# A gated mix of a state-space scan and an MLP: the last output tile's stores, dealt out anew to two DMA queues

## The chip, the cores and the metric

The kernel runs on one core of one Trainium2 chip. The metric is the device time in microseconds of one execution; lower is better. Before the change it is 136.66 us, the median of three runs (136.61 to 136.97).

## The reference, cut to what matters

For one sequence of 2048 rows with 448 columns, the reference computes a state-space branch `a` (a complex diagonal recurrence with 448 states along the sequence, then an output projection), an MLP branch `b` (448 to 1792 and back, SiLU between), and mixes them row by row with a sigmoid gate:

```python
x = A_x
g = _sigmoid((x * gate_w).sum(-1, keepdims=True))
a = _A_ref(x, ...)   # h[t] = Lam_bar * h[t-1] + x[t] B_bar ;  y = 2 Re(C h) + x * Dskip
b = _B_ref(x, w1, w2)   # silu(x @ w1) @ w2
return g * a + (1 - g) * b
```

The output is bfloat16 of shape (1, 2048, 448), written row by row.

## The kernel before, in words

The sequence is treated as 1024 pairs of rows: `x2` and `out2` are views of 1024 x 896, where columns 0 to 447 are the even row of a pair and 448 to 895 the odd one. A block `kt` is 128 pairs, so there are 8 blocks and 16 output tiles `tile = 2 * kt + odd` of 128 partitions x 448 columns.

Every instruction is recorded by a small helper, the `Tracker`: `T.op` records a compute instruction, `T.dma` a transfer. Both work out, from the names of the buffers that an instruction reads and writes, which semaphores it has to wait for. The order on each engine is the order of these calls, written out by hand; there is no scheduler. Each transfer has a semaphore of its own. `T.wait_all("sp", outs)` at the end makes the SyncE (SP) engine wait for all output stores in the order in which they were recorded, and nothing comes after it. A transfer can be issued by SP's queue or by ScalarE's (`"act"`); ScalarE's own instructions and the transfers that it issues stand in one order.

The first part of the kernel loads the inputs, computes the MLP and the scans, and keeps the states in `HS` and `VE`. Then come the 16 output tiles. For each one:

- `yseed` (line 1041) lets ScalarE copy a start value into a bank of PSUM.
- `yhalf` (line 1049) adds seven matmuls of the states with the projection `CO`, `YA` five of them and `YB` two.
- `yout` (lines 1062 to 1079) applies the gate and adds the MLP's share, and stores the tile. For the first eight tiles (`kt < 4`) that is a ScalarE activation (line 1070), for the last eight a VectorE operation (`scalar_tensor_tensor`, line 1073). The result lies in one of eight output buffers; the profile names four of them `OT` and the other four `TMPS`. The store is line 1077.

Fifteen tiles are stored whole, by one transfer each on SP's queue. The sixteenth, the last one (`kt = 7`, even), is cut by columns: a first piece of 280 columns and a second of 168. Each piece has its own bank, its own seven matmuls, its own VectorE operation and its own store. The rule for the queue is in `yout`: a piece that begins at column 0 goes to `"sp"`, the other to `"act"`. The loop that does this stands at line 1225, right ahead of the final wait.

Of the kernel before, what the change touches and what calls it, by code (L numbers as in the profile page):

```python
# [19 lines left out]
D = 448  # L20
# [130 lines left out]
def gated_mix(nc, A_x, A_Lambda_re, A_Lambda_im, A_B_re, A_B_im, A_C_re, A_C_im, A_log_dt,  # L151
              A_Dskip, B_x, B_w1, B_w2, gate_w, out):
    with ExitStack() as ctx:
        E = ctx.enter_context
        T = Tracker(nc, ctx)

        def sb(name, shape, dtype):
            return E(nc.sbuf_tensor(name, list(shape), dtype))

        x2 = A_x[0].rearrange("(k i) d -> k (i d)", i=2)  # L160
        out2 = out[0].rearrange("(k i) d -> k (i d)", i=2)
# [16 lines left out]
        OT = sb("OT", [128, 4, D], BF16)  # L178
# [21 lines left out]
        def bs(tile):  # L200
            kt, odd = tile // 2, tile % 2
            if odd:
                return BT[:, :, :].rearrange("p j n -> p (j n)")[:, kt * D:(kt + 1) * D]
            if kt > 3:
                return (COS, SIN)[kt // 6][:, 0, (kt % 2) * D:(kt % 2 + 1) * D]
            return IOTA[:, :].bitcast(BF16)[:, kt * D:(kt + 1) * D]
# [6 lines left out]
        def xg(b):  # L213
            if b < 2:
                return CO[:, 4 * b:4 * b + 4, :], [f"CO{m}" for m in (range(4) if b == 0 else range(4, 7))]
            if b == 2:
                return OT[:, 0:4, :], [f"OT{i}" for i in range(4)]
            v = TMPS[:, :, :].rearrange("p a b -> p (a b)").bitcast(BF16)
            return v[:, 0:4 * D].rearrange("p (k c) -> p k c", k=4), [f"TMP{i}" for i in range(3)]
# [90 lines left out]
        for i, src in enumerate((A_B_re, A_B_im)):  # L310
# [12 lines left out]
            out=ID[:, :], in_=ID[:, :], pattern=[[-1, 128]], compare_op=ALU.is_equal, fill=0.0,  # L323
            base=0, channel_multiplier=1), reads=["ID"], writes=["ID"])
        T.op("pool", lambda e: e.iota(IOTA[:, :].bitcast(I32), pattern=[[1, NK]], base=0, channel_multiplier=0),
             writes=["IOTA"])
# [128 lines left out]
        def ffn1(c, f0=0, ahead=None):  # L455
            for fb in range(f0, NFB, 2):
                pair(*ffn1_pair(c, fb), last=(c == 3 and fb == NFB - 2))
                if ahead and fb == 8:
                    ahead()
                yield  # L460
# [58 lines left out]
        for k in (2, 3):  # L519
# [7 lines left out]
            reads=["pv", "ps7"], writes=["PV"])  # L527
# [30 lines left out]
        def pact(o, a, f, ra, scale=1.0, bias=0.0):  # L558
# [22 lines left out]
            reads=["f2"] + SGN, writes=["f2s"])  # L581
# [84 lines left out]
        for n in (32, 64):  # L666
            T.op("dve", lambda e, n=n: e.tensor_copy(GD[n:2 * n, :, :], GD[0:n, :, :]), reads=["GW", "DB"],
                 writes=["GW", "DB"])
# [7 lines left out]
             writes=["BTz"] + BTK[2:4])  # L676
# [361 lines left out]
        def yseed(kt, odd):  # L1038
            bank, tile = nxt(), 2 * kt + odd
            s = bs(tile) if kt < 4 else xd(tile)  # L1040
            T.op("act", lambda e: e.activation(ps[:, bank, 0:D], s, AF.Copy),
                 reads=[f"BS{tile}" if kt < 4 else f"XD{block(tile)}"], writes=[f"ps{bank}"])
            seeds.append((kt, odd, bank))

        def yhalf(ms, kt, odd, bank, c=slice(0, D)):
            def mm(pe):
                ins = None
                for m in ms:
                    ins = pe.matmul(ps[:, bank, c], state(kt, odd, m), CO[:, m, c], start=False, stop=(m == YB[-1]),  # L1049
                                    skip_group_check=True)  # L1050
                return ins
            T.op("pe", mm, reads=sk(kt, odd, ms) + [f"CO{m}" for m in ms], writes=[f"ps{bank}"])
            return kt, odd, bank
# [5 lines left out]
            yhalf(YB, kt, odd, bank)  # L1059
            return 2 * kt + odd, bank  # L1060

        def yout(tile, bank, c=slice(0, D)):
            kt, odd = tile // 2, tile % 2
            i = n_o[0] % 8
            n_o[0] += c.stop == D
            o = (OT[:, i, :] if i < 4 else xg(3)[0][:, i - 4, :])[:, c]
            extra = xg(3)[1] + ["CT4", "CT5", "CT6"] if n_o[0] == 5 else []
            g = GT[:, 1, tile:tile + 1]
            if kt < 4:
                T.op("act", lambda e: e.activation(o, ps[:, bank, 0:D], AF.Copy, scale=g),  # L1070
                     reads=[f"ps{bank}", "GT1_0"], writes=[f"OT{i}"] + extra)
            else:
                T.op("dve", lambda e: e.scalar_tensor_tensor(  # L1073
                    o, ps[:, bank, c], g, bs(tile)[:, c], ALU.mult, ALU.add),
                    reads=[f"ps{bank}", "GT1_1", f"BS{tile}"], writes=[f"OT{i}_{c.start}"] + extra + (
                        [f"OT{i}"] if c.start == 0 else []))
            outs.append(T.dma("act" if c.start else "sp", lambda e: e.dma_start(
                out2[kt * 128:(kt + 1) * 128, odd * D + c.start:odd * D + c.stop], o),
                reads=[f"OT{i}" if kt < 4 else f"OT{i}_{c.start}"], writes=[f"out{tile}_{c.start}"]))

        outs = []

# [80 lines left out]
        f = ffn1(2)  # L1163
# [48 lines left out]
        for _ in range(8):  # L1212
            t = yclose(*yopen())
            ahead()
            yout(*t)
        run(s2)
        opened = [yopen(), yopen(), yopen()]
        kt, odd = tiles[-1]
        for n in range(1, 8):
            ahead()  # L1220
            yout(*yclose(*opened.pop(0)))
            if n in (2, 3, 4, 6):
                opened.append(yopen())
        yseed(kt, odd)
        for c in (slice(0, 280), slice(280, D)):
            kt, odd, bank = seeds.pop(0)
            yhalf(YA + YB, kt, odd, bank, c)
            yout(2 * kt + odd, bank, c)
        T.wait_all("sp", outs)

        T.emit()
# [2 lines left out]
def bass_gated_mix__ssm_conv_s5__dense_activation_silu__prompt_kernel(nc, *args):  # L1234
    gated_mix(nc, *args)
# [28 lines left out]
```

## Time and profile before

| What | Value |
|---|---|
| Time, median of 3 runs | 136.66 us (136.61 to 136.97) |
| Span of the profiled execution, first to last instruction | 135.2 us |
| TensorE clock granted | 1.000 |
| PE busy | 131.8 us, 97% of the span |
| DVE (VectorE) busy | 115.6 us, 86% |
| ACT (ScalarE) busy | 93.8 us, 69% |
| POOL (GpSimd) busy | 15.9 us, 12% |
| Output stores on SP's queue | 16 (15 of 112 KB, one of 70 KB) |
| Output stores on ScalarE's queue | 1 of 42 KB |
| Issue to landing of these stores, median | 1.6 to 1.7 us |

The profile is one execution. The page gives its span, which runs from the first to the last instruction of any engine, waits included; it gives no total for that execution beside it. So the profiled execution's own time is the 135.2 us of the span, and the difference to the 136.66 us of the runs' median is what lies around it. PE is a matmul on TensorE, PEld a weight load, SPq and ACTq are transfers issued by the two queues. The issue of a transfer is an instruction with a duration; "landing" is when its semaphore has been counted up by all DMA engines.

### The profile page before, as it was taken

The page shows a single profiled execution, that of the slowest core. Times are in us where ns is not written, and L with a number is a line of the kernel's source. Part 1 is how long each engine was busy: PE and PEld are TensorE (multiplying, and loading weights), DVE is VectorE, ACT ScalarE, POOL GpSimd, SP SyncE. Part 2 cuts the span into 40 slices and gives each one's busy share as a digit, 9 for nine tenths or more (in the row PEclk, how much of TensorE's full clock was granted, in tenths as well). Part 3 has the DMA queues.
Part 4 walks back from the last instruction along what each step waited for, and adds up shares of the span by engine and source line. Part 5 has one row for each costly group of instructions (what it writes and reads, how often), then busy time and mean ns, then how long its engine had stood idle before and what let it go on. Part 6 is the DMA issues. An engine that isn't in the chain of part 4 may idle for free.

```text
span 135.2 us, 2632 instructions
## 1 busy us (share of the span) xinstructions
PE 131.8 (97%) x1072; PEld 65.4 (48%) x1073; DVE 115.6 (86%) x154; ACT 93.8 (69%) x146; POOL 15.9 (12%) x32
## 2 busy tenths in 40 slices
PE   7899999999999999999999999999999999999993
PEld 7444444444444554444445544445555555555552
DVE  1369999917899798999999999999999999994554
ACT  0459888899939999769999597797114437879200
POOL 7108349650000000000000000000000000000000
DMA  4999979898997220000222000000000000322123
GB/s 110 259 275 176 125 140 264 165 323 248 259 188 119 53 63 0 0 0 0 55 47 58 5 0 0 0 5 0 0 0 0 0 0 5 102 91 79 68 80 124
DMA packets 24736, 11.78 MB, mean 87 GB/s; under 512 B 16851, under 2 KB 24214, under 8 KB 24726
## 3 DMA queue, kind: packets, MB, share of 16 engines
q1 hardware_dynamic: 22996, 10.43, 33.4%
q10 hardware_dynamic: 1730, 1.20, 3.1%
q8 instruction: 8, 0.13, 0.4%
q14 instruction: 2, 0.02, 0.0%
HBM read 5.34 MB, written 1.84 MB: 53 GB/s over the span
## 4 chain that ended last, share of the span: by engine, by line
PE 94%; DMA 2%; DVE 1%; SPq 1%; issue 0%
PE ps L362 44%; PE ps L796 16%; PE ps L811 16%; PE ps L1049 15%; PE ps L430 3%; DMA XN<-in_A_x_dram 2%; PE ps L488 1%; DVE TMPS L1073 1%; SPq L226 1%; PE ps L444 1%; PE ps L469 0%
## 5 line engine op out<-in xcount | busy, mean ns | idle before, releaser
L362 PE MATMUL ps<-XT,W1E 64*128 64x512 bf16 x325 | 41.3, 376 | 0.0
L452 ACT ACTIVATE AT<-ps 128x1024 bf16<-128x1024 f32 x28 | 28.2, 1020 | 7.4 <-PE ps L362 7.2
L362 PEld LDWEIGHTS ps<-XT,W1E 64*128 64x128 bf16 x325 | 16.9, 94 | 19.1 <-ACT AT L452 0.3
L362 PE MATMUL ps<-XT,BT 64*128 64x512 bf16 x156 | 22.4, 376 | 0.0
L811 PE MATMUL ps<-W,AT 64*128 64x448 bf16 x224 | 21.5, 349 | 0.0
L796 PE MATMUL ps<-W,AT 128*128 128x448 bf16 x112 | 21.4, 353 | 0.0
L796 PEld LDWEIGHTS ps<-W,AT 128*128 128x128 bf16 x112 | 10.9, 98 | 10.5 <-issue 0.4
L811 PEld LDWEIGHTS ps<-W,AT 64*128 64x128 bf16 x224 | 10.9, 94 | 10.4
L840 ACT ACTIVATE BT<-ps,GT 128x448 bf16<-128x448 f32 x8 | 5.1, 634 | 13.2 <-PE ps L796 13.2
L896 DVE SCALAR_TENSOR_TENSOR HS<-VE,P,ps 128x512 bf16<-128x512 bf16 (+1 forms) x13 | 9.6, 781 | 3.8 <-PE ps L362 3.8
L362 PEld LDWEIGHTS ps<-XT,BT 64*128 64x128 bf16 x156 | 8.1, 94 | 9.4 <-DVE HS L896 0.4
L940 DVE TENSOR_TENSOR_SCAN G<-P,Q 128x1024 f32<-128x1024 f32 (+1 forms) x6 | 11.4, 1922 | 0.0
L1049 PE MATMUL ps<-CO,VE 128*128 128x448 bf16 (+2 forms) x63 | 11.1, 332 | 0.0
L1049 PE MATMUL ps<-CO,HS 128*128 128x448 bf16 x56 | 11.1, 352 | 0.0
L362 PE MATMUL ps<-XR,W1E 64*128 64x512 bf16 x25 | 9.2, 376 | 0.0
L1049 PEld LDWEIGHTS ps<-CO,VE 128*128 128x128 bf16 x63 | 6.0, 98 | 4.8
L1049 PEld LDWEIGHTS ps<-CO,HS 128*128 128x128 bf16 x56 | 5.5, 98 | 5.1
L893 DVE TENSOR_TENSOR Q<-G,COS 128x2048 bf16<-128x2048 f32 (+1 forms) x4 | 7.0, 1756 | 0.1
L893 DVE TENSOR_TENSOR Q<-G,SIN 128x2048 bf16<-128x2048 f32 (+1 forms) x4 | 7.0, 1752 | 0.0
L858 ACT ACTIVATE VE<-ps 128x1024 bf16<-128x1024 f32 x6 | 6.1, 1020 | 1.2 <-PE ps L362 1.2
L860 ACT ACTIVATE ps<-VE,P 128x1024 f32<-128x1024 bf16 x6 | 6.7, 1118 | 0.2
L896 DVE SCALAR_TENSOR_TENSOR VE<-HS,P,FP 128x512 bf16<-128x512 bf16 (+1 forms) x7 | 6.6, 977 | 0.1
(124 smaller groups left out, 181.0 us busy)
## 6 DMA issues: line engine op xcount, KB each, us to landing
W<-in_B_w_dram SPq DMA_DIRECT2D x2, 784.0 KB, 6.3
XN<-in_A_x_dram SPq DMA_DIRECT2D x1, 896.0 KB, 5.5
out_dram<-OT SPq DMA_DIRECT2D x8, 112.0 KB, 1.7
out_dram<-TMPS SPq DMA_DIRECT2D x7, 112.0 KB, 1.7
HS<-HS SPq DMA_DIRECT2D x4, 128.0 KB, 2.3
XN<-in_A_x_dram SPq DMA_DIRECT2D x1, 384.0 KB, 3.6
W1E<-in_B_w_dram SPq DMA_DIRECT2D x1, 256.0 KB, 5.6
W1E<-in_B_w_dram ACTq DMA_DIRECT2D x1, 256.0 KB, 5.6
```

The costliest lines, as they stand in the source:

```text
L362: ins = pe.matmul(ps[:, bank, :], w(p, j), xh(odd, h, j, p), start=start and j == js[0], stop=stop and j == js[-1], skip_group_check=seeded)
L430: T.op("pe", lambda pe, fb=fb, bank=bank, j=j, h=h, c=c: pe.matmul(ps[:, bank, c], W1E[:, j, ff(fb) * 128:(ff(fb) + 1) * 128], XT[:, j, c] ...
L452: T.op("act", lambda e: e.activation(a[:, fb:fb + n, :], ps[:, bank:bank + n, :], AF.Silu), reads=[f"ps{bank + i}" for i in range(n)], wri ...
L796: ins = pe.matmul(ps[:, bank, 0:D], a[:, fb, q * 128:(q + 1) * 128], W2[:, ff(fb), :], start=(first and fb == 0), stop=(fb == NFB - 1), sk ...
L811: ins = pe.matmul(ps[:, bank, 0:D], a[p, fb, q * 128:(q + 1) * 128], W2[p, ff(fb), :], start=(start and fb == 0), stop=(not start and fb = ...
L840: T.op("act", lambda e: e.activation(bs(tile), ps[:, bank, 0:D], AF.Copy, scale=sc), reads=[f"ps{bank}", "GT2" if h else "GRI"], writes=ks)
L858: T.op("act", lambda e: e.activation(VE[:, m:m + 2, hs], ps[:, b[0]:b[0] + 2, :], AF.Copy), reads=[f"ps{i}" for i in b], writes=vs)
L860: T.op("act", lambda e: e.activation(ps[:, o[0]:o[0] + 2, :], VE[:, m:m + 2, hs], AF.Copy, scale=c1("lr", pt)), reads=vs + ["lr"], writes= ...
L893: T.op("dve", lambda e: e.tensor_tensor(o, a, b, op), reads=reads, writes=writes)
L896: T.op("dve", lambda e: e.scalar_tensor_tensor(o, a, s, b, ALU.mult, ALU.add), reads=reads, writes=writes)
L940: T.op("dve", lambda e: e.tensor_tensor_scan(G[:, c, w], rb, Q1[:, c, w], init, ALU.mult, ALU.add), reads=[f"Q1{c}", "rr", f"G{c}"], write ...
L1049: ins = pe.matmul(ps[:, bank, c], state(kt, odd, m), CO[:, m, c], start=False, stop=(m == YB[-1]), skip_group_check=True)
```

## The change

The function that stores a tile takes a list of transfers, each with a queue and a range of rows; without it a tile is stored whole by SP's queue. For the last tile the list is given: its first piece (280 columns) is one transfer on ScalarE's queue, and its second (168 columns) is two transfers, rows 0 to 63 on SP's queue and rows 64 to 127 on ScalarE's. Both halves read what one VectorE operation writes, and wait for it. Each of the three has its own semaphore, and the final wait takes them in this order.

```diff
-        def yout(tile, bank, c=slice(0, D)):
+        def yout(tile, bank, c=slice(0, D), to=(("sp", 0, 128),)):
...
-            outs.append(T.dma("act" if c.start else "sp", lambda e: e.dma_start(
-                out2[kt * 128:(kt + 1) * 128, odd * D + c.start:odd * D + c.stop], o),
-                reads=[f"OT{i}" if kt < 4 else f"OT{i}_{c.start}"], writes=[f"out{tile}_{c.start}"]))
+            for eng, r0, r1 in to:
+                outs.append(T.dma(eng, lambda e, r0=r0, r1=r1: e.dma_start(
+                    out2[kt * 128 + r0:kt * 128 + r1, odd * D + c.start:odd * D + c.stop], o[r0:r1, :]),
+                    reads=[f"OT{i}" if kt < 4 else f"OT{i}_{c.start}"], writes=[f"out{tile}_{c.start}_{r0}"]))
...
-        for c in (slice(0, 280), slice(280, D)):
+        for c, to in ((slice(0, 280), (("act", 0, 128),)), (slice(280, D), (("sp", 0, 64), ("act", 64, 128)))):
             kt, odd, bank = seeds.pop(0)
             yhalf(YA + YB, kt, odd, bank, c)
-            yout(2 * kt + odd, bank, c)
+            yout(2 * kt + odd, bank, c, to)
```

## The prediction

> **What bounds the kernel now.** I read the chain of waits first, then the timeline of the last three microseconds, then busy time by stretch behind the last compute instruction. The page's chain:
>
> ```profile
> ## 4 chain that ended last, share of the span: by engine, by line
> PE 94%; DMA 2%; DVE 1%; SPq 1%; issue 0%
> ```
>
> TensorE sets the pace of nearly the whole span. The change touches no matmul and no VectorE instruction, so only the tail behind PE can move. The timeline from 132.5 us on (start, duration, queue or engine, line):
>
> ```profile
> 132.26 0.91 PE L1049 MATMUL ps<-CO,VE 128*128 128x280 bf16 x9
> ...
> 132.58 0.99 SPq L1077 DMA_DIRECT2D out_dram<-TMPS  x2
> 132.70 0.90 DVE L1073 SCALAR_TENSOR_TENSOR TMPS<-ps,GT,SIN 128x280 bf16<-128x280 f32 x2
> 133.63 0.38 ACTq L1077 DMA_DIRECT2D out_dram<-TMPS  x1
> ```
>
> PE ends at 133.17. The two VectorE pieces (280 and 168 columns, 0.51 and 0.39 us) run back to back to 133.60. SP issues the first piece's store at 133.24 (the second of its x2), ScalarE's queue the second's at 133.63. That is the last instruction of any engine that does work; the remaining 1.6 us are one DMA's way to DRAM, and SP waits for it:
>
> ```profile
> L1077 ACTq DMA_DIRECT2D out_dram<-TMPS x1: 379/379/379, 133.6 to 133.6; - x1
> ...
> DMA to landing us min/median/max: 1.6/1.6/1.6
> ```
>
> How these 1.6 us are made up, in five stretches (stretch, length, five engines' busy time, clock, DMA share, GB/s):
>
> ```profile
> 134.00:134.05 0.05, 0.00 (x0) 0.00 (x0) 0.00 (x0) 0.00 (x0) 0.00 (x0) 1.00 0.00 0
> 134.05:134.45 0.40, 0.00 (x0) 0.00 (x0) 0.00 (x0) 0.00 (x0) 0.00 (x0) 1.00 0.61 179
> 134.45:134.51 0.06, 0.00 (x0) 0.00 (x0) 0.00 (x0) 0.00 (x0) 0.00 (x0) 1.00 0.00 0
> 134.51:134.83 0.32, 0.00 (x0) 0.00 (x0) 0.00 (x0) 0.00 (x0) 0.00 (x0) 1.00 0.56 135
> 134.83:135.23 0.40, 0.00 (x0) 0.00 (x0) 0.00 (x0) 0.00 (x0) 0.00 (x0) 1.00 0.00 0
> ```
>
> The second stretch holds the first piece's packets (70 KB), the fourth the second's (42 KB), with silence between: the two stores don't meet. The last store is a **lead** of 0.88 us from issue to first packet (133.63 to 134.51), 0.32 us of **packets**, and a silent 0.40 us of **tail** until SP's wait ends at 135.23. Only 0.32 of 1.60 us is moving bytes. That is what splitting the store can shorten; lead and tail are paid by each half.
>
> **The change, part by part.** Two stores become three. The matmuls, the two VectorE pieces and all earlier stores stay in place: no cost, and nothing in the sum.
>
> First piece moves from SP's queue to ScalarE's. It waits for VectorE's first piece as before (133.21) and starts at 133.24. ScalarE's last activation ends at 127.08 (126.53 + 0.55), and behind this store its queue holds only the half store, so the new wait holds up nothing else. Landing, at 133.24 + 1.6 = 134.9, stays ahead of the end. The cost on the path is that its issue of 0.38 us keeps ScalarE's queue until 133.62, and the next issue starts some 0.035 us behind (at the kernel's start ScalarE's queue issues at 0.78 for 0.425 us and again at 1.24). So ScalarE's half starts at 133.66 instead of 133.63: **+0.02 us**, rounded, if the first issue is not slowed. SP, which loses that store, is free from 132.91 on.
>
> The halves. A half has 64 rows of 336 bytes. The packet records give 8 data packets of about 20 ns for each of the 16 DMA engines in the whole store; a half has 4, so its packets take 4 x 0.02 = 0.08 us less, 0.24 instead of 0.32: **-0.08 us** if the other half doesn't interfere. SP's half: issue 133.63, lead 0.83 (packet records of SP's stores on line 1077), packets 0.24, tail 0.40: 135.10. ScalarE's half: 133.66 + 0.88 + 0.24 + 0.40 = **135.18**. It is the later one, 0.05 ahead of 135.23. SP's wait list grows by one; the six waits at 133.62 to 133.96 come every 0.06 us while SP sits waiting anyway, so this costs nothing unless both halves land within that time, and then at most 0.06.
>
> Sharing the DMA engines: if both halves' packets serialised wholly, 128 data packets plus one more round of 4-byte completion packets (about 10 ns) take 0.33 us from SP's first packet at 134.46, and 134.79 + 0.40 = 135.19, against 135.18. So this term is 0.01 us either way, because the starts are already 0.08 apart. The Trainium skill, "DMA: Bandwidth & Descriptors", in its rules for kernel authors, speaks against this change: it says not to bother with two transfers to disjoint partition halves, since both spread over the same 16 engines. By it the packet gain is lost but for the earlier start, and the sum below would end at 135.26 instead of 135.25.
>
> What before does not show is a store of 64 rows, nor two stores issued together. **Two queues at once** is shown at the start of the kernel only:
>
> ```profile
> 0.78 0.39 SPq L226 DMA_DIRECT2D XN<-in_A_x_dram  x1
> 1.24 0.42 SPq L226 DMA_DIRECT2D W1E<-in_B_w_dram  x1
> ```
>
> ```profile
> 0.78 0.42 ACTq L226 DMA_DIRECT2D XN<-in_A_x_dram  x1
> 1.24 0.45 ACTq L226 DMA_DIRECT2D W1E<-in_B_w_dram  x1
> ```
>
> Each pair starts within 5 ns, and each issue is 0.05 to 0.09 longer than the single stores' 0.33 and 0.38. The packet records put the first packet of the first pair 1.02 (SP) and 1.17 us (ScalarE's queue) behind the issue, against 0.83 and 0.88: +0.19 and +0.29. Those are the core's first loads and read DRAM, so I take the lengthening of the issue, **+0.07 us**, as my value, and 0 and +0.29 as ends. **64 rows** are shown by the partition swaps of line 992 (SBUF to SBUF, 2048 bytes a row):
>
> ```profile
> L992 SPq DMA_DIRECT2D Q<-Q x2: 462/537/612, 65.7 to 66.2; - x2
> ```
>
> ```profile
> 66.17:66.78 0.61, 0.61 (x10) 0.26 (x8) 0.61 (x2) 0.61 (x2) 0.00 (x0) 1.00 0.00 0
> ```
>
> The first is issued at 65.67 in 0.462 us, 0.13 more than a store of 128 rows, and no packet moves before 66.78: a lead of 1.11, 0.28 longer. On the other side, the one-row load at 3.02 was issued in 0.22, 0.11 less than 0.33; a half may thus be issued faster than the whole. Ends: -0.11 and +0.28. The nearest row is the store itself: 560-byte and 896-byte rows have one lead (0.83), so its kind sets the lead rather than its size, and I take **0** for the rows.
>
> Sum: +0.02 - 0.08 + 0.07 = +0.01; with the 0.01 of sharing, +0.02 us. The span goes from 135.23 to about 135.25. What lies around the span is 136.66 - 135.23 = 1.43 us, by the median of the runs (136.61 to 136.97; the profiled execution has no total of its own on the page). None of it is touched: **136.68 us**.
>
> **The rivals.** (1) *The halves run clean.* Nothing is lost to simultaneous issue: 135.18, so 136.61; with the faster issue of few rows (-0.11) 135.07, so 136.50. For it: the lead didn't change with bytes, and SP's half has 0.08 us of slack. Against: the start of the kernel. Lead and tail make 1.28 of the 1.60 us, so even a half without any packets would save 0.32: a gain over 0.41 us has no place in this tail.
>
> (2) *One queue's issue holds the other's; slower.* Both halves are released by the same VectorE end (133.60), so they ask for descriptors at the same moment, and before they didn't: its two last issues were 0.39 apart. If the second is held for the whole issue of the first, ScalarE's half begins at 133.63 + 0.33 = 133.96 and ends at 133.96 + 0.88 + 0.24 + 0.40 = 135.48: 136.91, +0.25. If 64 rows cost as in the swaps (hold 0.46, lead 0.28 longer), it ends at 133.63 + 0.46 + 1.16 + 0.24 + 0.40 = 135.89: 137.32, +0.66. It counts as slower once hold and longer lead exceed 0.48 us together (0.41 + 0.05 of gain + 0.02 of start already in it). Against full holding: the pair at 0.78 took 0.39 and 0.425, where one behind the other would show some 0.7 in one of them. The Trainium skill, "Perfetto Trace Analysis", "DMA Instruction — HWDGE", has this as a rule: the descriptor generator is shared and locked for exclusive use, and the time waiting for the lock is inside the issue's recorded duration. By that rule the trace agrees only in part.
>
> (3) *The lengthening of both kinds without holding.* Lead +0.29 and rows +0.28 on ScalarE's half: 135.18 + 0.57 = 135.75, 137.18.
>
> That the change doesn't do what it says is excluded by the order of the built instructions: ScalarE's queue gains a 128x280 store and a 64x168 store in place of 128x168; SP's last one is 64x168; PE and VectorE are the same.
>
> **How the numbers follow.** 0.3% (0.41 us), about what a measurement of this kernel can tell from no change, is larger than most of these cases. Forecast, ends within 0.15 us of before: 0.47. Rival 1: 0.17. Rival 2: 0.26, over half of it beyond 0.41, since its ends are 0.25 and 0.66 and the start's rows speak for less. Rival 3: 0.10, nearly all beyond. A late landing is a risk of every store (of the stores on line 1077 the one issued at 115.31 landed after 2.6 us, the others after 1.6 to 1.8), and one store more at the end is part of the slower side. Faster by over 0.3% is left 0.05, for what lies around the span or a shorter tail. Within 0.3%: 0.47 + 0.13 (rival 1 less what goes to faster) + 0.11 (rival 2's lower end) = 0.71; slower 0.24. The range goes from 136.45 (rival 1's 136.50 less 0.05, the lowest run's distance from the median) to 137.15, short of the far ends of rivals 2 and 3.
>
> **What would show it.** Right: in the after-profile ScalarE's queue has stores at about 133.24 and 133.66, SP's last at 133.63; both halves' issues last 0.33 to 0.47; packets run from about 134.5 in one stretch to 134.85; the span ends at 135.1 to 135.4. Rival 1: issues of 0.33 or less and a span under 135.15. Rival 2: one half's issue lasting 0.6 or more, or its first packet 0.3 us behind the other's. Rival 3: both leads over 1.1. Wrong altogether: any PE or VectorE instruction moved before 133.6, a tail longer than 0.40, or a changed difference between span and total.

## The result, and the profile after

The change makes the kernel slower by a third of a per cent: 137.19 us (median of 22 runs, 136.64 to 137.79) against 136.66 us (22 runs), a ratio of 1.0032 with a 95% interval of 1.0021 to 1.0043, or 0.44 us of 136.66 (0.29 to 0.59). The two plain medians stand further apart, 0.53 us; the ratio with its interval is what this text goes by. The forecast was 136.68, with a range up to 137.15: by the ratio the time is 137.10, just inside it, and the plain median lies 0.04 us above it.

The span of the profiled execution, 135.42 us, is only 0.19 above that of before. The timeline shows why a span misleads here (start, duration, queue or engine, line):

```profile
132.26 1.56 SPq L1078 DMA_DIRECT2D out_dram<-TMPS  x2
...
132.38 0.90 DVE L1073 SCALAR_TENSOR_TENSOR TMPS<-ps,GT,SIN 128x280 bf16<-128x280 f32 x2
...
132.92 0.97 ACTq L1078 DMA_DIRECT2D out_dram<-TMPS  x2
```

VectorE's last piece ends at 133.28 here and ended at 133.60 before. That 0.32 us was there long before the change's place: the first output store started at 113.99 before and at 113.67 now. Over all the profiles of this study VectorE's end lies between 133.26 and 133.92. So what the change costs has to be measured from VectorE's last end to the end of the span. From here on this time is called the tail; the prediction used the word for the silent 0.40 us behind the last packet alone. By the trace's records the tail was 135.233 - 133.600 = **1.633 us** before and is 135.418 - 133.280 = **2.138 us** now: +0.505, which is the loss that the runs show, within their interval's reach (up to 0.59).

The three stores start where they should, 0.36 us before VectorE's end (first piece, ScalarE's queue), 0.03 (SP's half) and 0.06 behind it (ScalarE's half). ScalarE's half by itself, its issue in ns and its way to landing:

```profile
L1078 ACTq DMA_DIRECT2D out_dram<-TMPS x1: 556/556/556, 133.3 to 133.3; - x1
...
DMA to landing us min/median/max: 2.0/2.0/2.0
```

Before, the store that ended last took 379 ns and 1.6 us. The stretches behind VectorE's end (stretch, length, five engines, clock, DMA share, GB/s):

```profile
133.28:133.80 0.52, 0.00 (x0) 0.00 (x0) 0.00 (x0) 0.00 (x0) 0.00 (x0) 1.00 0.34 114
133.80:134.17 0.37, 0.00 (x0) 0.00 (x0) 0.00 (x0) 0.00 (x0) 0.00 (x0) 1.00 0.65 194
134.17:134.46 0.29, 0.00 (x0) 0.00 (x0) 0.00 (x0) 0.00 (x0) 0.00 (x0) 1.00 0.00 0
134.46:134.75 0.29, 0.00 (x0) 0.00 (x0) 0.00 (x0) 0.00 (x0) 0.00 (x0) 1.00 0.41 74
134.75:135.03 0.28, 0.00 (x0) 0.00 (x0) 0.00 (x0) 0.00 (x0) 0.00 (x0) 1.00 0.41 77
135.03:135.42 0.39, 0.00 (x0) 0.00 (x0) 0.00 (x0) 0.00 (x0) 0.00 (x0) 1.00 0.00 0
```

The second stretch is the first piece. Then nothing moves for 0.29 us, where 0.06 were silent before. The fourth stretch is SP's half and the fifth ScalarE's: the packet records put SP's last packet's end at 134.750 and ScalarE's first at 134.752. The halves neither overlap nor take half the time: each needs 0.26 to 0.28 us for 64 packets, where the whole store needed 0.30 for 128. SP's half had a lead (issue to first packet) of 1.16 us instead of 0.83, ScalarE's 1.41 instead of 0.88.

### The profile page after: what moved, and what is told of

It is laid out like the page before. It is cut to its first block, busy times and chain, and to the rows that moved or that the text cites. A ratio compares the mean times of both kernels' runs of the same rounds, so it can differ in the third digit from the quotient of the medians.

```text
span 135.4 us, 2633 instructions
## 1 busy us (share of the span) xinstructions
PE 131.4 (97%) x1072; PEld 65.5 (48%) x1073; DVE 115.6 (85%) x154; ACT 93.8 (69%) x146; POOL 15.9 (12%) x32
## 4 chain that ended last, share of the span: by engine, by line
PE 94%; DMA 2%; DVE 1%; SPq 0%; issue 0%
PE ps L362 44%; PE ps L796 16%; PE ps L811 16%; PE ps L1049 15%; PE ps L430 3%; DMA W1E<-in_B_w_dram 2%; PE ps L488 1%; DVE TMPS L1073 1%; PE ps L444 1%; SPq L226 0%; PE ps L469 0%
```

## The experiments

The tail is always the time from VectorE's last end to the end of the span; leads, from issue to first packet, are from the packet records.

**1. The first piece on ScalarE's queue, the second whole on SP's.**

```diff
-(slice(280, D), (("sp", 0, 64), ("act", 64, 128)))
+(slice(280, D), (("sp", 0, 128),))
```

> One part of the change alone: the first piece (280 columns) on ScalarE's queue, the second whole, 128 rows, on SP's. The measure is the time from the end of VectorE's last piece to the end of the span: 1.63 us before the change, 2.14 after it. Theory A (a store of 64 rows is itself dearer) and theory B (two stores issued at the same moment hold each other up) both expect that nothing is lost here: issue 0.33, first packet 0.83 behind the issue, 0.32 of packets, 0.40 of tail, together 1.55 to 1.60, and a time within 0.1 us of before. Theory C (the first piece on ScalarE's queue is what costs, because its packets or its landing come later) expects 1.8 or more.

```profile
133.22 0.37 ACTq L1078 DMA_DIRECT2D out_dram<-TMPS  x1
133.61 0.33 SPq L1078 DMA_DIRECT2D out_dram<-TMPS  x1
```

Tail 1.592, lead 0.85; ratio to before 0.9997 (0.9979 to 1.0014). Theory C falls: moving the first piece costs nothing. The whole store from SP's queue ends 0.04 us earlier than before, 0.03% of the time, which these runs cannot tell from none.

**2. The second piece halved by columns, at 364.** Two stores of 128 rows x 84 columns at the same moment; the list gets column bounds.

```diff
-(slice(280, D), (("sp", 0, 64), ("act", 64, 128)))
+(slice(280, D), (("sp", 0, 128, 280, 364), ("act", 0, 128, 364, D)))
```

> The second piece is halved by columns instead of rows: two stores of 128 rows x 84 columns, one on SP's queue, one on ScalarE's, issued at the same moment; first piece on ScalarE's queue as in the change. Theory A expects no loss: issues of 0.33 and 0.33 to 0.38, leads of 0.83 to 0.88, 1.55 to 1.65 us from VectorE's last end to the span's end. Theory B expects the loss of the change or most of it: issues of 0.5 or more, ScalarE's first packet 0.3 us behind SP's, 1.9 to 2.2 us.

Both theories missed. SP's half was untouched (issue 0.333, lead 0.84), ScalarE's a little slower (0.445 and 0.95), yet the tail was 2.066 and the ratio 1.0039 (1.0024 to 1.0054). The loss lies behind the last packet:

```profile
134.68:135.09 0.41, 0.00 (x0) 0.00 (x0) 0.00 (x0) 0.00 (x0) 0.00 (x0) 1.00 0.60 105
135.09:135.89 0.80, 0.00 (x0) 0.00 (x0) 0.00 (x0) 0.00 (x0) 0.00 (x0) 1.00 0.00 0
```

A silent 0.80 us where 0.40 is usual is a loss of another kind than the change's, so this kernel doesn't decide between A and B by its time. By its leads, theory B is worth 0.07 us here. Experiment 7 takes up the rest.

**3. ScalarE's half alone.**

```diff
-(slice(280, D), (("sp", 0, 64), ("act", 64, 128)))
+(slice(280, D), (("act", 64, 128),))
```

> Left out: rows 0 to 63 of the second piece are not stored, so SP issues nothing at the end; ScalarE's queue stores the first piece and then rows 64 to 127 of the second, with nobody beside it. Theory A expects ScalarE's half as dear as in the change or nearly: issue 0.50 or more instead of 0.38, lead 1.15 to 1.40 us, 1.9 to 2.1 us from VectorE's last end to the span's end. Theory B alone expects issue 0.33 to 0.38, lead 0.83 to 0.88, packets 0.24, 1.5 to 1.6 us. If both have a share, A's part is lead 1.16 (SP's half had 1.16 in the change) and the end at about 1.85.

```profile
L1078 ACTq DMA_DIRECT2D out_dram<-TMPS x1: 554/554/554, 133.7 to 133.7; - x1
...
DMA to landing us min/median/max: 1.8/1.8/1.8
```

With nobody beside it, the half is issued in 554 ns, as in the change (556), with a lead of 1.21 us against 0.88 for 128 rows. Tail 1.941. So 0.31 of the 0.505 us belong to the half itself (theory A), and the other 0.20 need SP's half: ScalarE's lead is 1.41 with it and 1.21 without. This is one profile; experiment 5 tests the row count on more stores.

**4 and 5. Ladders of row counts.** The first left two stores in a row on one queue, and they backed up: the packets of the store at 115.3, which also lands late before the change, came late; the next issue lasted 1.47 us, and most later stores followed close behind one another. Only three of its first stores were clean.

```diff
+cuts = [(0, 128), (0, 64, 128), (0, 32, 128), (0, 96, 128), (64, 128, 0, 64), (0, 112, 128), (0, 16, 128), (0, 80, 128)]
...
-yout(*t)
+yout(*t, to=tuple(("sp", p, q) for p, q in zip(x, x[1:]) if q > p))
```

> The end is as before the change. Of the first eight tiles, which are 1.3 us apart and off the path at the end, the second to eighth are stored in two stores one behind the other on SP's queue, nothing on the other queue; rows of the first store: 64, 32, 96, 64 (the upper half first), 112, 16, 80. The first of each pair is issued by a queue that had nothing to do. Theory A expects issue and lead to depend on the rows alone: over 0.45 and 1.1 us at 64 against 0.33 and 0.83 at 128; if descriptors are made row by row the cost should fall with fewer rows (0.2 at 16), if any store of fewer than 128 rows takes a slower way all seven should show 0.45 or more. Theory B expects 0.33 and 0.83 or less for all of them.

The clean ones were 64 rows (issue 0.504, lead 1.16), 16 rows (0.315, 0.81) and 80 rows (0.317, 0.82). That already went against a price on every store of fewer than 128 rows. The second ladder has one store a tile:

```diff
+some = iter([(0, 128), (0, 128), (0, 64), (64, 128), (0, 32), (0, 96), (0, 112), (0, 48),
+             (0, 128), (0, 128), (0, 80), (0, 16), (32, 96), (0, 128), (0, 128)])
```

> Left out: of eight tiles only some rows are stored, one store each on SP's queue, which has nothing else to do for 0.4 us or more before it, and nothing on the other queue: rows 0-63, 64-127, 0-31, 0-95, 0-111, 0-47 (tiles three to eight), 0-79, 0-15, 32-95 (tiles eleven to thirteen); the end is as before the change. Theory A1 (a store of exactly 64 rows is dear) expects issue about 0.50 and lead about 1.16 us for the three stores of 64 rows and 0.32 to 0.34 and 0.80 to 0.84 for all others; in the ladder with two stores a tile the clean 16 and 80 rows had 0.315 and 0.317. Theory A2 (any store of fewer than 128 rows is dear) expects 0.45 or more for all nine. Theory A3 (the cost depends on where the rows lie) expects the three of 64 rows to differ from each other.

The two stores of 64 rows (x2: shortest, median and longest issue in ns):

```profile
L1078 SPq DMA_DIRECT2D out_dram<-OT x2: 484/495/506, 117.0 to 118.3; - x2
...
DMA to landing us min/median/max: 1.9/1.9/1.9
```

The same view over the four stores of 32, 96, 112 and 48 rows:

```profile
L1078 SPq DMA_DIRECT2D out_dram<-TMPS x4: 314/330/347, 119.6 to 123.6; - x4
...
DMA to landing us min/median/max: 1.5/1.6/1.8
```

The leads, by the second store of 64 rows (issued at 118.28) and the one of 96 (at 120.93):

```profile
118.55:119.41 0.86, 0.86 (x6) 0.49 (x5) 0.86 (x2) 0.61 (x2) 0.00 (x0) 1.00 0.00 0
119.42:119.84 0.42, 0.42 (x4) 0.20 (x2) 0.42 (x1) 0.42 (x2) 0.00 (x0) 1.00 0.58 137
120.93:121.76 0.83, 0.83 (x6) 0.39 (x4) 0.83 (x1) 0.58 (x2) 0.00 (x0) 1.00 0.00 0
121.77:122.26 0.49, 0.49 (x4) 0.29 (x3) 0.45 (x2) 0.49 (x2) 0.00 (x0) 1.00 0.67 176
```

Packets begin at 119.42, 1.14 us behind the issue of 64 rows, and at 121.77, 0.84 behind that of 96. Rows 0-63, 64-127 and 32-95 had leads of 1.16, 1.14 and 1.24; 16, 32, 48, 80, 96 and 112 rows had 0.81 to 0.85, at issues of 0.31 to 0.35. The first of the three stands right behind the late store of 115.6, where whole stores also took up to 0.60 us to issue in other profiles, so the weight lies on the other two. Theory A1 holds: of the counts tried, exactly 64 rows is dear, wherever they lie. Why is not shown.

A whole store issued at 131.82, 0.62 us behind the third of them on the same queue, was slow as well: issue 0.587 and lead 1.08, where one that followed a whole store by 0.59 us (at 127.44) had 0.350 and 0.85.

**6. The change, cut at row 80.**

```diff
-(("sp", 0, 64), ("act", 64, 128))
+(("sp", 0, 80), ("act", 80, 128))
```

> The change with the rows of the second piece cut at 80 instead of 64: 80 rows on SP's queue, 48 on ScalarE's. Theory A1 expects SP's lead at 0.83 (1.16 in the change) and ScalarE's at 0.88 plus what the two issues cost each other: 0.08 to 0.20 by theory B, 0 without it; from VectorE's last end to the span's end 1.60 (no B) to 1.80 us, and a time 0.3 to 0.5 us under the change's, within 0.15% of before. Theory A2 expects 2.1 us and a time 0.3% above before.

```profile
L1078 SPq DMA_DIRECT2D out_dram<-TMPS x1: 343/343/343, 133.5 to 133.5; - x1
L1078 ACTq DMA_DIRECT2D out_dram<-TMPS x1: 443/443/443, 133.5 to 133.5; - x1
...
DMA to landing us min/median/max: 1.5/1.6/1.7
```

Leads 0.85 and 0.95, tail 1.755, ratio 1.0004 (0.9990 to 1.0018). One number in the source, 64 to 80, removes 0.38 of the 0.505 us, and by the runs the loss is gone. What stays, 0.12 us over before, is ScalarE's lead (+0.07) and its way from the last packet to the landing (0.45 us instead of 0.37), less the shorter packets. Where ScalarE's packets ran beside SP's and ended last, as here and in experiment 7, that way took 0.45 us; where they came behind SP's, as in the change, 0.36.

**7. Column halves at 384, a multiple of 256 bytes in a row.**

```diff
-(("sp", 0, 128, 280, 364), ("act", 0, 128, 364, D))
+(("sp", 0, 128, 280, 384), ("act", 0, 128, 384, D))
```

> The second piece halved by columns again, but at column 384 (byte 768 of a row's 896) instead of 364 (byte 728): 104 columns on SP's queue, 64 on ScalarE's, all 128 rows. In the cut at 364 the leads were 0.84 and 0.95, but ScalarE's store needed 0.81 us from its last packet to the end where all others needed 0.40. If that is because the two stores write bytes of the same small block of DRAM, the tail is back at 0.40 here and the end 1.65 to 1.75 us behind VectorE's last end. If narrow rows (128 bytes now) or two stores in flight make the tail, it stays at 0.7 or more and the end at 2.0 or more. ScalarE's lead should again be 0.95, 0.08 more than alone, by theory B.

Leads 0.85 and 0.95; from ScalarE's last packet to its last landing 0.45 us, where the cut at 364 had 0.77; tail 1.738, inside the expected 1.65 to 1.75. Narrower rows (128 bytes instead of 168) did not bring the long silence back, so narrowness is out as its cause. That the two stores write bytes of one small block fits, but one profile of each cut, which also differ in the width of both stores, doesn't show it; the cause stays open.

**8. The first piece back on SP's queue.**

```diff
-(slice(0, 280), (("act", 0, 128),))
+(slice(0, 280), (("sp", 0, 128),))
```

> The first piece back on SP's queue, the two halves of 64 rows as in the change. If the halves carry the loss, the end is as late as in the change: 2.0 to 2.2 us from VectorE's last end, ratio about 1.003. ScalarE's half can start 0.03 us earlier than in the change, SP's as early as there. If the first piece on ScalarE's queue has a share in ScalarE's lead of 1.41 us (its descriptors still being worked on), that lead falls to 1.2 and the end to 1.95.

With the first piece on SP's queue the leads are 1.16 (SP) and 1.42 (ScalarE), the tail 2.126, the ratio 1.0039 (1.0019 to 1.0059). The halves carry the whole loss; the first piece has no share in ScalarE's wait.

**9 and 10. Who waits for whom.** With the aligned column cut, 64 rows on one queue and 128 on the other.

```diff
-(("sp", 0, 128, 280, 384), ("act", 0, 128, 384, D))
+(("sp", 0, 64, 280, 384), ("act", 0, 128, 384, D))      # experiment 9
+(("sp", 0, 128, 280, 384), ("act", 64, 128, 384, D))    # experiment 10
```

> Left out: rows 64 to 127 of columns 280 to 383 of the last tile. The aligned column cut with 64 rows on SP's queue (104 columns) and all 128 rows on ScalarE's (64 columns), issued at the same moment. Theory B1 (the queue that comes second begins only when the first store's descriptors are done, and 64 rows take longest to make) expects ScalarE's lead at 1.10 to 1.20 us, though its own store is of the cheap kind, and its first packet at the moment of SP's last. Theory B2 (two queues cost each other a fixed 0.08, and the 0.20 of the change belong to two stores of 64 rows meeting) expects 0.95 as in the column cuts. SP's lead is 1.16 in both.

> Left out: rows 0 to 63 of columns 384 to 447 of the last tile. The mirror image: 128 rows on SP's queue (104 columns), 64 rows on ScalarE's (64 columns), at the same moment. Theory B1 expects ScalarE's lead at 1.21 (the half alone) plus the 0.07 to 0.08 that a cheap store on SP cost it in the column cuts: 1.28 to 1.30, and 0.2 us between VectorE's last end and the span's end less than in the change, about 1.95 to 2.05. Theory B2 expects the same 1.29; if instead the queues' meeting costs 0.20 whenever a store of 64 rows is on ScalarE's side, it is 1.41 and 2.1.

Experiment 9, then experiment 10:

```profile
L1078 SPq DMA_DIRECT2D out_dram<-TMPS x1: 507/507/507, 133.4 to 133.4; - x1
L1078 ACTq DMA_DIRECT2D out_dram<-TMPS x1: 445/445/445, 133.4 to 133.4; - x1
```

```profile
L1078 SPq DMA_DIRECT2D out_dram<-TMPS x1: 333/333/333, 133.8 to 133.8; - x1
L1078 ACTq DMA_DIRECT2D out_dram<-TMPS x1: 552/552/552, 133.8 to 133.8; - x1
```

In 9 ScalarE's lead is 0.95, as beside a store of 128 rows, and its packets begin before SP's: theory B1 falls, a slow store on SP does not hold ScalarE's cheap one. In 10 ScalarE's lead is 1.21, just that of the half alone and not the 1.28 to 1.30 that both theories expected, and the tail is 1.863, shorter than the expected 1.95 to 2.05: here the queues' meeting costs the 64-row store nothing. So of the pairs tried, the extra 0.20 us appears only where two stores of 64 rows meet, in the change and in experiment 8. There their first packets are 0.28 and 0.27 us apart, near the 0.33 us that such a store needs extra: it is as if that extra work were done for one store at a time. What that work is, no run here shows.

## Why the prediction was right or wrong

The forecast was +0.02 us, no change that can be measured. The tail grew by 0.505 us, and by the runs the time grew by 0.44, just over the 0.41 that the prediction took as the bound. That 137.10 still lies inside the range is luck: the range reached so far up because of the rivals, while the sum had 0.07 us for the two terms, rows and queues, that measured 0.53. By its own steps:

- **The place was right.** No matmul and no VectorE instruction moved in order, and the whole difference lies behind VectorE's last end.
- **The first piece's move** was put at +0.02 us for ScalarE's later start: 0.025 measured (0.027 in the half alone), and nothing else (experiments 1 and 8).
- **64 rows** was the step that failed. Between the ends -0.11 and +0.28 I took 0, because the lead hadn't changed with the bytes of a row. The row count is another thing than the row's bytes, and the view of before that the prediction itself shows of 64 rows, the partition swap, had the price: lead 1.11 there, 1.14 to 1.24 in stores. Measured: **+0.33 us**, even over the upper end. The reason given for preferring the stores' rows ("its kind sets the lead") excluded exactly what the trace showed.
- **Two queues at once** was put at +0.07, ends 0 and +0.29. For stores of other row counts that was right (0.07 in the lead, experiments 2, 6, 7 and 9). For two stores of 64 rows it is **+0.20**, and beside a store of 128 rows a 64-row store lost nothing (experiment 10).
- **The packets** were to shrink by 0.08 us, half of eight packets at 20 ns. They shrank by 0.04 (0.304 to 0.263). A packet took 26 ns instead of 21, so the four of one engine 0.10 us, and the 16 DMA engines don't run in step: by the completion packets the first was through at 134.85 and the last at 135.02.
- **Sharing the DMA engines**, 0.01, played no part, since the halves didn't meet.
- **Around the span**, 1.43 us came from the median of the runs and the span of one execution. The profiled execution of the change took 136.94 us, 1.52 more than its span, and the other profiled ones lie between 1.24 and 1.56, so a change of 0.1 us in it says nothing.

The sum as measured: 0.025 + 0.333 + 0.201 - 0.041 - 0.013 (a slightly shorter silence behind the last packet) = 0.505 us, the growth of the tail.

The profile of before also had a nearer row than the ones that the prediction used: two loads of 64 rows, issued 0.03 us apart on the two queues at 3.745 and 3.775, in 0.572 and 0.562 us. The pairs of 128 rows at 0.78 and 1.24 took 0.39 to 0.45. That is a hint and no more, since many loads were under way by then, and later loads of 128 rows (at 4.37 and 5.70) took 0.84 and 0.60 us.

Of the rivals, the third, lengthening of both kinds without holding, priced at +0.57 in the lead, comes nearest in size: 0.33 + 0.20 = 0.53. Its mark, both leads over 1.1, is what the trace shows. It had a chance of 0.10, rival 2 had 0.26. Rival 2's picture, a wait for the other queue's issue, shows in part: ScalarE's first packet came 0.28 us behind SP's, close to its mark of 0.3, and as SP's packets ended. But this wait of 0.20 us is not inside the recorded issue (556 ns with SP's half, 554 without), where the Trainium skill's page "Perfetto Trace Analysis" ("DMA Instruction — HWDGE") has it, and experiments 9 and 10, where only one of the two stores has 64 rows, show none of it. Only the 0.07 us of the other stores lies inside the issue (445 ns against 379). Rival 1, clean halves, happened nowhere; the nearest to it is the cut at row 80, 0.12 us behind before.

The rule of the Trainium skill in "DMA: Bandwidth & Descriptors" (rules for kernel authors), not to bother with two transfers to disjoint partition halves, gave the right advice. Its reason, that both use the same 16 DMA engines, is not what cost the time here: the cut at 80 shares the same engines, its two stores' packets overlap for 0.20 us, and it is level with before by the runs.

## What to carry to other kernels

The last store of this kernel was mostly lead and the silence behind its last packet, 1.28 of 1.60 us, and a split shortens neither: look at what a split can save (0.04 us) before asking what it may cost. When a change makes an instruction of a shape that the profile has elsewhere, price it by that shape's row, even if it does other work, and not by the row of the same purpose. When two executions differ before the place of the change, measure from the last event that both share.

## What the runs showed of the hardware

- On SP's queue a store of exactly 64 partitions was issued in 0.48 to 0.58 us and moved its first packet 1.14 to 1.24 us after the issue's start; stores of 16, 32, 48, 80, 96, 112 and 128 partitions needed 0.31 to 0.35 us and 0.81 to 0.85 us when no store was close ahead of them (the first two output stores, of 128 partitions, 0.37 to 0.39 and 0.87 to 0.89). On ScalarE's queue it was 0.55 and 1.21 against 0.38 and 0.88. Two stores of 64 partitions at the same moment on the two queues put another 0.20 us on the second. Why 64 is dear is not shown.
- Two stores whose rows meet at byte 728 had their last landing 0.77 us behind the last packet (one profile), against 0.45 with the border at byte 768 and 0.37 for the second piece stored whole; the cause is not shown.
